# Fused Fourier mixing and MLP mixer on one Trainium2 core: re-planning the setup and moving the Nyquist column from TensorE to VectorE

## The chip, the cores and the metric

One core of a Trainium2 chip. The metric is the device time of one execution in microseconds (us). The profile is one execution; its "span" runs from the first to the last instruction and is about 1.8 us shorter than the device time of the same execution. The kernel's matrix products run on TensorE (PE in the profile, PEld is its weight loads), the copies, adds and activations on VectorE (DVE), ScalarE (ACT) and GpSimd (POOL). GpSimd and SyncE (SP) also issue the data transfers.

Executions differ, mostly by 1 to 2 us, by up to 3.5 us for the kernel before (642.22 to 645.68). The profiles below point to TensorE's granted clock in the first 50 us; that it explains every such difference is not shown, since only one execution of each run was profiled.

## The reference

```
X = fft(fft(x, axis=1), axis=2).real            # x: 8 x 3008 x 256
h = relu(X.transpose(0,2,1) @ w_tok1) @ w_tok2  # w_tok1: 3008 x 256, w_tok2: 256 x 3008
u = X + h.transpose(0,2,1)
out = u + relu(u @ w_ch1) @ w_ch2               # w_ch1: 256 x 1536, w_ch2: 1536 x 256
```

## The kernel before

All eight batches go through the core one after the other. The work of a batch has two parts.

- The **front** computes the Fourier transform and the token products: z products (short transforms along the sequence), the d stage (the transform along the 256 features, 12 groups), the token products with w_tok1 already carried through the transform tables (tiles hp and hq), the third stage (py, pq) and the products with w_tok2 (pu). It ends in the tile ut.
- The **channel part** has 24 sub-steps per batch. Each is one group of first channel products (mm1: six products of 512 columns) and one of second channel products (mm2: twelve of 256 columns).

The front of batch b+1 is a generator whose steps are handed out between the sub-steps of batch b by a plan. Before all this there is a **setup**: angle tables tp and tq (sines), small tables for z (t1n, t1b) and for the d stage (td0, td1), the load of the first batch x0 and its **fold** on VectorE (sums and differences of mirrored rows), and hp and hq.

The order of the setup, shortened:

```python
    r3 = []
    for off in (offp, offq):                         # angles of tp and tq, both on VectorE
        m3 = gen.tile([P, 768], FP32, ...)
        ts(m3[:], kb[:], reff[:], AT.mult, off[:], AT.add)
        r3.append(reduced(m3[:], S, P, 768))          # three more VectorE operations
    table3(tp, r3[0]); turn(tp, tts_p, 12)            # sines on ScalarE, transposes on TensorE
    table3(tq, r3[1]); turn_rows(tts_p, 1.0, 8)
    pl = nc.gpsimd
    ...                                               # t1n, t1b: on GpSimd (eng=pl)
    turn(tq, tts_q, 24); turn_rows(tts_q, -1.0, 0)
    ...                                               # td0, td1, perm: on GpSimd
    load_wc()
    take(fold(0, [nc.vector] * 4), 4)
    x_tiles[1] = load_x(1)
    own = front(0)
    take(own, 4); carried(tts_p, hp)                  # carried: 24 products with w_tok1
    take(own, 4); carried(tts_q, hq)
    take(own, 19)                                     # d stage, token products, third stage, first pu
```

The d stage and the third stage, in `front(b)`:

```python
        for g in range(NG):                           # NG = 12
            pw = ps_f("pw")                           # one of three PSUM buffers
            ...
            nc.tensor.matmul(pw[:, 0:WD], lhsT=zb, rhs=td1[:], start=True, stop=False)   # 259 columns
            nc.tensor.matmul(pw[:, 0:131], lhsT=za, rhs=td0[:], start=False, stop=True)
            copy(g % 2 and b == 0, w[:, g, :], pw[:, 0:WD])
            yield
        ...
        for c in range(3):                            # third stage, all chunks ahead of pu
            ...
            yield
```

The plan, and the end of the last batch in `mm2` (ks counts the four row blocks of a chunk):

```python
    plan = [[0] * 11 + [3, 3, 2, 4, 4, 4, 1, 1, 2, 1, 4, 4, 4], ...]   # steps of the next front per sub-step
    ...
        if ks % 2 == 0:
            box["po"] = ps_out("po")                  # one PSUM tile for two row blocks
        ...
        if ks % 2 == 1:                               # VectorE adds for two blocks at once
            ...
        if ks == 3:                                   # stores for four blocks
```

## Time and profile before

| | before |
|---|---|
| time, three runs | 642.7 us (642.53 to 643.55) |
| PE busy | 618.1 us, 96% of the span |
| first channel product starts | 44.57 us |
| batch 0, to batch 1's first channel product | 79.87 us |
| one batch, mean from batch 2 to batch 7 | 74.54 us |
| from batch 7's start to the end of the span | 71.68 us |

From the page of the profile: busy time by engine, the tenths of TensorE's busy time and granted clock in 40 slices, and the chain of work that ended last.

```profile
PE 618.1 (96%) x4778; PEld 425.6 (66%) x4778; DVE 330.4 (51%) x702; ACT 317.4 (49%) x667; POOL 251.0 (39%) x250
PE   3789999999999999999999999999999999999996
PEclk9779999999999999999999999999999999999999
PE 93%; POOL 2%; DVE 2%; ACT 1%; issue 1%; DVEq 0%; POOLq 0%; ACTq 0%
```

TensorE bounds the kernel, and only the first three slices (48 us) and the last show anything else. The view of stretches says it sharper. Its columns are the stretch, its length, then busy time of PE, PEld, DVE, ACT and POOL (number of instructions in brackets), the granted clock, the share of the DMA engines and GB/s.

```profile
40.00:50.00 10.00, 8.82 (x34) 3.62 (x34) 6.76 (x12) 4.63 (x9) 2.98 (x2) 0.66 0.80 178
140.00:600.00 460.00, 460.00 (x3564) 318.05 (x3563) 233.01 (x487) 224.82 (x483) 148.53 (x130) 1.00 0.41 78
```

Between 140 and 600 us TensorE is never idle, so there only TensorE work that is taken away can save time. At 40 to 50 us its mean clock is 0.66.

A caution for every clock figure. The clock records of a profile begin when the clock is first raised, 13.5 to 25.5 us into the span in the profiles here. Ahead of that the views print 1.00, but the spacing of the products shows half clock. In the kernel before the first record is at 13.48 us, and twelve products of 128 columns take 1.46 us ahead of it and 0.83 us after it:

```profile
9.85 1.46 PE L266 MATMUL pt<-ident,tp 128*128 128x128 f16 x12 [9.85 <-ACT tp L235]
...
14.03 0.83 PE L266 MATMUL pt<-ident,tq 128*128 128x128 f16 x12
```

So a mean clock of 1.0 over a whole span speaks only of the time after the first record.

TensorE in the timeline: start, length, engine, line, operation, tiles. First a d group (two products) in the steady part and the first product of the next, then the first channel products, then the last 48 products of the kernel.

```profile
138.05 0.27 PE L443 MATMUL pw<-td_305,z 128*128 128x259 f16 x1
138.16 0.22 PE L444 MATMUL pw<-td_304,z 128*128 128x131 f16 x1
138.22 0.27 PE L443 MATMUL pw<-td_305,z 128*128 128x259 f16 x1
...
44.57 2.88 PE L539 MATMUL pc<-ut,wc1p 128*128 128x512 f16 x6 [0.43 <-DVE ut L514]
...
631.57 5.40 PE L560 MATMUL po<-wc_148,c_7866 128*128 128x256 f16 x48
```

Lengths of products overlap; the distance between starts is what a product costs: 0.11 us for 259 columns and 0.06 us for 131. The six first channel products take 2.88 us, where later ones take 1.46: that is the half clock.

VectorE in the timeline, the start and end of the fold of x0:

```profile
11.10 0.68 DVE L394 TENSOR_TENSOR xd<-xp,xm 94x1024 f16<-94x1024 f16 x1
11.81 0.69 DVE L395 TENSOR_TENSOR xp<-xp,xm 94x1024 f16<-94x1024 f16 x1
...
20.00 0.58 DVE L403 TENSOR_TENSOR eo<-xd 94x635 f16<-94x635 f16 x1
```

### The profile page before, as it was taken

How to read it: one execution, taken by the hardware profiler on the slowest of the kernel's cores; microseconds unless marked ns; L12 is line 12 of the kernel's file. 1: busy time of each engine (PE TensorE's matmuls, PEld its weight loads, DVE VectorE, ACT ScalarE, POOL GpSimd, SP SyncE). 2: the span in 40 equal slices, each digit the busy share in tenths (PEclk: the TensorE clock that was granted, in tenths of full speed). 3: DMA queues.
4: the chain of work that ended last, by engine and by line, in shares of the span. 5: the costliest groups of instructions: out<-in, count | busy, mean ns of one | idle time of the engine just before them, and what ended most of it. 6: DMA issues, size and time to landing. Idle time of an engine off the chain costs nothing.

```text
span 642.6 us, 11805 instructions
## 1 busy us (share of the span) xinstructions
PE 618.1 (96%) x4778; PEld 425.6 (66%) x4778; DVE 330.4 (51%) x702; ACT 317.4 (49%) x667; POOL 251.0 (39%) x250
## 2 busy tenths in 40 slices
PE   3789999999999999999999999999999999999996
PEld 3545667567666776667766676667766777666665
DVE  8755435733664447633565336643466336653442
ACT  7547465265535554365534645356533655334431
POOL 8819869659130880059411691039400000000000
PEclk9779999999999999999999999999999999999999
DMA  9992462732922268142853239323221522533332
GB/s 148 177 215 52 92 140 51 149 60 55 161 67 67 58 93 149 33 101 56 130 74 78 66 61 140 82 66 83 58 51 34 115 51 50 67 74 70 80 82 66
DMA packets 86550, 56.28 MB, mean 88 GB/s; under 512 B 54832, under 2 KB 83440, under 8 KB 85744
## 3 DMA queue, kind: packets, MB, share of 16 engines
q1 hardware_dynamic: 78240, 38.04, 28.5%
q0 software_dynamic: 8256, 17.49, 17.1%
q8 instruction: 37, 0.61, 0.4%
q14 instruction: 17, 0.14, 0.1%
HBM read 34.98 MB, written 24.64 MB: 93 GB/s over the span
## 4 chain that ended last, share of the span: by engine, by line
PE 93%; POOL 2%; DVE 2%; ACT 1%; issue 1%; DVEq 0%; POOLq 0%; ACTq 0%
PE po L560 38%; PE pc L539 38%; PE pu L506 6%; PE pw L443 2%; PE pz L416 1%; PE pw L444 1%; PE py L482 1%; PE pq L482 1%; PE ph L363 0%; DVE yt L487 0%; DVE ut L514 0%; PE ph L365 0%; PE pz L432 0%; POOL xm L118 0%; PE pz L426 0%
## 5 line engine op out<-in xcount | busy, mean ns | idle before, releaser
L539 PE MATMUL pc<-ut,wc1p 128*128 128x512 f16 x576 | 141.3, 381 | 0.5 <-DVE ut L514 0.4
L539 PE MATMUL pc<-ut,wc1m 128*128 128x512 f16 (+1 forms) x576 | 134.9, 370 | 0.0
L574 DVE TENSOR_TENSOR osb<-po,rt 128x258 f32<-128x258 f32 (+3 forms) x240 | 74.6, 361 | 55.9 <-PE po L560 51.5
L539 PEld LDWEIGHTS <-wc1m 128*128 128x128 f16 x576 | 54.8, 98 | 54.0
L539 PEld LDWEIGHTS <-wc1p 128*128 128x128 f16 x576 | 53.2, 98 | 51.8 <-issue 5.7
L514 DVE TENSOR_TENSOR ut<-pu,yt 128x512 f16<-128x512 f32 (+1 forms) x96 | 61.5, 670 | 35.6 <-PE pu L506 35.6
L394 POOL TENSOR_TENSOR xd<-xp,xm 94x1024 f16<-94x1024 f16 x28 | 59.3, 2119 | 19.7 <-DMA xm<-in_x_dram,ix_76 19.7
L395 POOL TENSOR_TENSOR xp<-xp,xm 94x1024 f16<-94x1024 f16 x28 | 59.3, 2119 | 2.2
L399 POOL TENSOR_TENSOR eo<-xp 94x512 f16<-94x512 f16 (+1 forms) x28 | 34.0, 1213 | 61.6 <-PE pz L432 60.3
L291 ACT ACTIVATE w<-pw 128x259 f16<-128x259 f32 x90 | 30.1, 386 | 49.6 <-PE pw L444 49.1
L291 ACT ACTIVATE z<-pz 128x480 f16<-128x480 f32 (+1 forms) x59 | 34.5, 674 | 24.7 <-PE pz L416 20.5
L506 PE MATMUL pu<-w2p,uu 128*128 128x512 f16 (+1 forms) x168 | 45.0, 379 | 0.5 <-DVE ut L514 0.5
L487 DVE TENSOR_TENSOR yt<-py,qs 128x512 f16<-128x512 f32 x48 | 30.6, 685 | 18.9 <-ACT qs L485 9.4
L592 POOL COPY ch<-c_7196 128x768 f16<-128x768 f16 x1 | 0.8, 825 | 86.0 <-DVE c_7196 L87 86.0
L403 POOL TENSOR_TENSOR eo<-xd 94x508 f16<-94x508 f16 (+1 forms) x28 | 33.8, 1205 | 0.0
L506 PEld LDWEIGHTS <-uu 128*128 128x128 f16 x192 | 19.0, 99 | 11.7 <-issue 2.7
L485 ACT ACTIVATE qs<-pq 128x512 f32<-128x512 f32 x24 | 14.1, 595 | 19.4 <-PE pq L482 9.2
L443 PE MATMUL pw<-td_305,z 128*128 128x259 f16 x96 | 21.4, 274 | 0.9 <-ACT w L291 0.6
L594 POOL COPY c_7866<-ch 128x768 f16<-128x768 f16 x1 | 0.8, 828 | 50.8 <-PE po L560 50.8
L444 PE MATMUL pw<-td_304,z 128*128 128x131 f16 x96 | 18.8, 221 | 0.0
L474 ACT ACTIVATE uu<-uv 128x256 f16<-128x256 f32 (+2 forms) x48 | 13.2, 337 | 9.9 <-DVE uv L469 9.9
L128 POOL DMA_DIRECT2D xp<-in_x_dram x32 | 17.2, 561 | 0.2 <-issue 0.2
(429 smaller groups left out, 1146.8 us busy)
## 6 DMA issues: line engine op xcount, KB each, us to landing
out_dram<-osb SPq DMA_DIRECT2D x84, 256.0 KB, 3.7
xp<-in_x_dram POOLq DMA_DIRECT2D x16, 272.0 KB, 5.6
out_dram<-osb SPq DMA_DIRECT2D x12, 192.0 KB, 2.8
xp<-in_x_dram POOLq DMA_DIRECT2D x16, 127.5 KB, 6.2
rt<-ut SPq DMA_TRANSPOSE x96, 2.7
w2s<-in_moe_w_tok_dram POOLq DMA_DIRECT2D x1, 1504.0 KB, 18.3
w1p<-in_moe_w_tok_dram POOLq DMA_DIRECT2D x2, 384.0 KB, 9.6
wc_148<-in_moe_w_ch_dram POOLq DMA_DIRECT2D x1, 768.0 KB, 12.1
```

Of the source, the lines that this page charges most:

```text
L291: nc.scalar.activation(out=out_, in_=in_, func=AFT.Copy)
L394: eng.tensor_tensor(out=xd[:, t, :], in0=xp[:, t, :], in1=rv, op=AT.subtract)
L395: eng.tensor_tensor(out=xp[:, t, :], in0=xp[:, t, :], in1=rv, op=AT.add)
L399: eng.tensor_tensor(out=eo[:, t, 1:129], in0=xp[:, t, 1:129], in1=xp[:, t, 255:127:-1], op=AT.add)
L403: eng.tensor_tensor(out=eo[:, t, 129:256], in0=xd[:, t, 1:128], in1=xd[:, t, 255:128:-1], op=AT.subtract)
L443: nc.tensor.matmul(pw[:, 0:WD], lhsT=zb, rhs=td1[:], start=True, stop=False)
L487: nc.vector.tensor_tensor(out=yt[:, h, CW * c:CW * c + CW], in0=py[:], in1=qs[:], op=op)
L506: nc.tensor.matmul(pu[:, 0:n], lhsT=uu[:, th, int(minus), h, :], rhs=w2_cols(b, c)[:, th], start=(th == 0), stop=(th == 1))
L514: nc.vector.tensor_tensor(out=ut[:, h, f0:f0 + n].rearrange("p (a b) -> p a b", b=64), in0=pu[:, 0:n].rearrange("p (b a) -> p a b", b=64), ...
L539: nc.tensor.matmul(pc[:, 0:n], lhsT=wc[:, h, ct * P:(ct + 1) * P], rhs=ut[:, h, f0:f0 + n], start=(h == 0), stop=(h == 1))
L560: nc.tensor.matmul(po[0:n, o:o + D], lhsT=c1[:, ct, ks * P:ks * P + n], rhs=wc2[:, ct, :], start=(ct == 0), stop=(ct == NCT - 1))
L574: nc.vector.tensor_tensor(out=osb[r, ks_, j], in0=src[r, k0:k1, j], in1=rt[r, ks_, p], op=AT.add)
```

## The change

The intent has five parts.

1. **Nyquist by VectorE.** The d stage's first product had 259 columns only because one Nyquist value with alternating sign was added to 131 columns by the product. Now it has 128 columns, and VectorE adds the alternating row.
2. **Setup.** The small tables (t1n, t1b, td) go to VectorE, where they fill the wait for x0; the angles of tq go to GpSimd; the d stage is dealt out among the products with w_tok1.
3. **Clock.** 24 filler products stand ahead of the first channel product.
4. **Plan.** The third stage is made one chunk at a time, ahead of the pu products of its chunk; eleven steps of batch 1's front move from batch 0 into batch 1; half of a sub-step's steps go ahead of mm2.
5. **Tail.** In the last chunk of the last batch every row block is added by itself, and the stores go out in two halves on two queues.

The core of the diff (cuts marked `...`):

```diff
-    r3 = []
-    for off in (offp, offq):
-        ...
+    ts(m1[0:KR, 0:48], kf[0:KR, 0:48], qcol[0:KR, :], AT.mult, 47 / 4, AT.add)     # eng=pl dropped, as in
+    ...                                                                            # all small tables
+    table3(tp, angles3(offp, nc.vector))
+    ...                                                  # ident, anti, md, td0, td1, t1n, t1b on VectorE
+    r3q = angles3(offq, pl)                              # tq's angles on GpSimd
+    load_wc()
...
-            nc.tensor.matmul(pw[:, 0:WD], lhsT=zb, rhs=td1[:], start=True, stop=False)
-            nc.tensor.matmul(pw[:, 0:131], lhsT=za, rhs=td0[:], start=False, stop=True)
-            copy(g % 2 and b == 0, w[:, g, :], pw[:, 0:WD])
+            nc.tensor.matmul(pw[:, 131:WD], lhsT=zb, rhs=td1[:], start=True, stop=True)
+            nc.tensor.matmul(pw[:, 0:131], lhsT=za, rhs=td0[:], start=True, stop=True)
+            copy(0, w[:, g, 132:WD], pw[:, 132:WD])
+            nc.vector.scalar_tensor_tensor(
+                out=w[:, g, 0:131], in0=alt[:], scalar=pw[:, 131:132],
+                in1=pw[:, 0:131], op0=AT.mult, op1=AT.add)
...
+        final = last and b + 1 == BB
+        if ks % 2 == 1 or final:
...
+                parts = [(slice(0, n), ks % 2, ks % 2 + 1)]
...
+        if ks == 3 or (final and ks == 1):
...
+    take(fold(0, [nc.vector] * 4), 4)
+    own = front(0)
+    take(own, 2)
+    filler(16)
+    table3(tq, r3q)
+    take(own, 2)
+    turn(tq, tts_q, 0)
+    take(own, 2)
+    turn_rows(tts_q, -1.0, 0)
+    take(own, 2)
+    for g2 in range(NG // 2 + 1):
+        if g2 < NG // 2:
+            take(own, 2)
+            carried(tts_p, hp, g2, 0)
+        if g2 > 0:
+            carried(tts_q, hq, g2 - 1, g2 % 3 > 0)
+    take(own, 5)
+    filler(24)
...
+    plan = [[0] * 11 + [2, 2, 2, 2, 3, 3, 3, 3, 1, 1, 1, 2, 1],
+            [2] * 10 + [1, 1, 1, 2, 1, 2, 1, 2, 1, 1, 1, 1, 1, 1]]
...
+                if sub < 12:
+                    take(own, 1)
+                take(nxt, n // 2)
                 if prev is not None:
                     mm2(*prev, s, pbox)
...
+                take(nxt, n - n // 2)
```

More of the change, by code (lines that the diff above doesn't have):

```diff
@@ L235, in sin @@
         nc.scalar.activation(out=out_, in_=in_, func=AFT.Sin, scale=scale)
-    ident = const.tile([P, P], FP16, tag="ident")
-    anti = const.tile([P, P], FP16, tag="anti")
-    acol = pvec("acol")
-    ts(acol[:], pcol[:], -1.0, AT.mult, 127.0, AT.add)
-    ts(ident[:], jrow[:, 0:P], pcol[:], AT.is_equal)
-    ts(anti[:], jrow[:, 0:P], acol[:], AT.is_equal)
-    r3 = []
-    for off in (offp, offq):
-        m3 = gen.tile([P, 768], FP32, tag="m3", bufs=2, name="m3")
-        ts(m3[:], kb[:], reff[:], AT.mult, off[:], AT.add)
-        r3.append(reduced(m3[:], S, P, 768))
     def table3(tab, r):
@@ L263, in turn @@
         for h in range(2):
-            pt = ps_f("pt", FP16, 1024)
+            pt = psum.tile([P, 1024], FP16, tag="mm", name="pt", bufs=3)
             for g in range(6):
@@ L291, in copy @@
             nc.scalar.activation(out=out_, in_=in_, func=AFT.Copy)
-    tts_p, tts_q = turned(), turned()
-    table3(tp, r3[0])
-    turn(tp, tts_p, 12)
-    table3(tq, r3[1])
-    turn_rows(tts_p, 1.0, 8)
     pl = nc.gpsimd
     mask0, q24 = pvec("mask0"), pvec("q24")
-    ts(mask0[:], xicol[:], -1.0, AT.mult, 1.0, AT.add, eng=pl)
-    ts(q24[:], qcol[:], 24.0, AT.add, eng=pl)
+    ts(mask0[:], xicol[:], -1.0, AT.mult, 1.0, AT.add)
+    ts(q24[:], qcol[:], 24.0, AT.add)
     t1n = const.tile([KR, 2, 2, 24], FP16, tag="t1n")
@@ L307 @@
     kf = krow[:].rearrange("p a k -> p (a k)")
-    ts(m1[0:KR, 0:48], kf[0:KR, 0:48], qcol[0:KR, :], AT.mult, 47 / 4, AT.add, eng=pl)
-    ts(m1[0:KR, 48:96], kf[0:KR, 48:96], qcol[0:KR, :], AT.mult, eng=pl)
-    ts(m1[0:KR, 96:120], kf[0:KR, 0:24], q24[0:KR, :], AT.mult, 47 / 8, AT.add, eng=pl)
-    r1 = reduced(m1[0:KR, :], 47, KR, 120, pl)
+    ts(m1[0:KR, 0:48], kf[0:KR, 0:48], qcol[0:KR, :], AT.mult, 47 / 4, AT.add)
+    ts(m1[0:KR, 48:96], kf[0:KR, 48:96], qcol[0:KR, :], AT.mult)
+    ts(m1[0:KR, 96:120], kf[0:KR, 0:24], q24[0:KR, :], AT.mult, 47 / 8, AT.add)
@@ L312, with angles3 @@
+    r1 = reduced(m1[0:KR, :], 47, KR, 120)
     cs = gen.tile([P, 120], FP32, tag="cs")
     sin(cs[0:KR, :], r1, PI2 / 47)
+    def angles3(off, eng):
+        m3 = gen.tile([P, 768], FP32, tag="m3", bufs=2, name="m3")
+        ts(m3[:], kb[:], reff[:], AT.mult, off[:], AT.add, eng=eng)
+        return reduced(m3[:], S, P, 768, eng)
+    table3(tp, angles3(offp, nc.vector))
+    ident = const.tile([P, P], FP16, tag="ident")
+    anti = const.tile([P, P], FP16, tag="anti")
+    acol = pvec("acol")
@@ new lines @@
+    ts(acol[:], pcol[:], -1.0, AT.mult, 127.0, AT.add)
+    ts(ident[:], jrow[:, 0:P], pcol[:], AT.is_equal)
+    ts(anti[:], jrow[:, 0:P], acol[:], AT.is_equal)
+    md = gen.tile([P, 255], FP32, tag="md")
+    ts(md[:, 0:128], jrow[:, 1:129], pcol[:], AT.mult, 64.0, AT.add)
+    ts(md[:, 128:255], jrow[:, 1:128], pcol[:], AT.mult)
+    rd = reduced(md[:], 256, P, 255)
+    td0 = const.tile([P, 131], FP16, tag="td0")
+    td1 = const.tile([P, P], FP16, tag="td1")
+    alt = const.tile([P, 131], FP16, tag="alt")
@@ L314 @@
+    sin(td0[:, 2:130], rd[:, 0:128], PI2 / 256)
+    sin(td1[:, 1:P], rd[:, 128:255], PI2 / 256)
     csv = cs[0:KR, 0:96].rearrange("p (a b k) -> p a b k", a=2, b=2)
     for i, m in ((0, mask0), (1, xicol)):
-        ts(t1n[:, :, i, :], csv[:, :, i, :], m[0:KR, :], AT.mult, eng=pl)
+        ts(t1n[:, :, i, :], csv[:, :, i, :], m[0:KR, :], AT.mult)
     ts(t1b[:, 1, :], cs[0:KR, 96:120], float(np.sqrt(0.5)), AT.mult,
-       xicol[0:KR, :], AT.mult, eng=pl)
-    pl.tensor_copy(out=t1b[:, 0:3:2, :], in_=t1n[:, :, 0, :])
@@ L321 @@
-    turn(tq, tts_q, 24)
-    turn_rows(tts_q, -1.0, 0)
-    md = gen.tile([P, 255], FP32, tag="md")
-    ts(md[:, 0:128], jrow[:, 1:129], pcol[:], AT.mult, 64.0, AT.add, eng=pl)
-    ts(md[:, 128:255], jrow[:, 1:128], pcol[:], AT.mult, eng=pl)
-    rd = reduced(md[:], 256, P, 255, pl)
-    td0 = const.tile([P, 131], FP16, tag="td0")
-    td1 = const.tile([P, WD], FP16, tag="td1")
-    sin(td0[:, 2:130], rd[:, 0:128], PI2 / 256)
-    sin(td1[:, 132:WD], rd[:, 128:255], PI2 / 256)
+       xicol[0:KR, :], AT.mult)
@@ L335 @@
+    nc.vector.tensor_copy(out=t1b[:, 0:3:2, :], in_=t1n[:, :, 0, :])
+    r3q = angles3(offq, pl)
+    load_wc()
     pl.memset(td0[:, 0:1], 1.0)
@@ L338 @@
     ts(td0[0:1, :], td0[0:1, :], 0.5, AT.mult, eng=pl)
-    pl.memset(td1[:, 0:132], 0.0)
-    pl.memset(td1[0:1, 0:2], 0.5)
-    pl.memset(td1[0:1, 3:130:2], 0.5)
-    pl.memset(td1[0:1, 2:130:2], -0.5)
+    pl.memset(td1[:, 0:1], 0.0)
+    pl.memset(td1[0:1, 0:1], 0.5)
+    pl.memset(alt[:], 1.0)
+    pl.memset(alt[:, 2:129:2], -1.0)
+    pl.memset(alt[:, 130:131], 0.0)
     tcol, sgn = pvec("tcol"), pvec("sgn")
@@ L351, with carried @@
     ts(perm[:], jrow[:, 0:P], tcol[:], AT.is_equal, sgn[:], AT.mult, eng=pl)
+    tts_p, tts_q = turned(), turned()
     hp = const.tile([P, NG, DTOK], FP16, tag="hp")
     hq = const.tile([P, NG, DTOK], FP16, tag="hq")
-    def carried(tts, dst):
-        for g2 in range(NG // 2):
-            ph = ps_mm("ph")
-            for k in range(2):
-                g = 2 * g2 + k
-                o = ph[:, k * DTOK:(k + 1) * DTOK]
-                nc.tensor.matmul(o, lhsT=tts[0][:, g * P:g * P + P], rhs=w1p[:, g, :],
-                                 start=True, stop=False)
-                nc.tensor.matmul(o, lhsT=tts[1][:, g * P:g * P + P], rhs=w1m[:, NG - 1 - g, :],
-                                 start=False, stop=True)
-            copy(g2 % 2, dst[:, 2 * g2:2 * g2 + 2, :].rearrange("p g k -> p (g k)"),
-                 ph[:])
+    def carried(tts, dst, g2, e):
+        ph = ps_mm("ph")
+        for k in range(2):
+            g = 2 * g2 + k
+            o = ph[:, k * DTOK:(k + 1) * DTOK]
+            nc.tensor.matmul(o, lhsT=tts[0][:, g * P:g * P + P], rhs=w1p[:, g, :],
+                             start=True, stop=False)
+            nc.tensor.matmul(o, lhsT=tts[1][:, g * P:g * P + P],
+                             rhs=w1m[:, NG - 1 - g, :], start=False, stop=True)
+        copy(e, dst[:, 2 * g2:2 * g2 + 2, :].rearrange("p g k -> p (g k)"), ph[:])
     w2v = w2s[:].rearrange("p h (b a) -> p h b a", a=NQ)
@@ L419, in front @@
                 zo = z[:, half, :, :].rearrange("p k (u s) -> p u k s", u=4)
-                copy(b == 0 and (half == 0 or t0 == 11), zo[:, :, :, t0:t0 + 5],
+                copy(b == 0 and t0 == 1, zo[:, :, :, t0:t0 + 5],
                      pz[:, 0:480].rearrange("p (t u k) -> p u k t", t=5, u=4))
@@ L476, in front, with third @@
         yt = perb.tile([P, 2, HALF], FP16, tag="yt", name="yt")
-        for c in range(3):
+        def third(c):
             py, pq = ps_f("py"), ps_f("pq")
@@ L488, in front @@
                                         in1=qs[:], op=op)
-            yield
         ut = perb.tile([P, 2, NCH * CW], FP16, tag="ut", name="ut", bufs=2)
@@ L499, in front @@
         for c in range(NCH):
+            if c < 3:
+                third(c)
+                yield
             f0 = CW * c
@@ L562, in mm2 @@
                              start=(ct == 0), stop=(ct == NCT - 1))
-        if ks % 2 == 1:
+        final = last and b + 1 == BB
+        if ks % 2 == 1 or final:
             src = po[:].rearrange("p (k d) -> p k d", k=2)
@@ L566, in mm2 @@
                                                           (slice(0, n), 1, 2)]
+            if final:
+                parts = [(slice(0, n), ks % 2, ks % 2 + 1)]
             for r, k0, k1 in parts[0:2 if n else 1]:
-                ks_ = slice(ks - 1 + k0, ks - 1 + k1)
+                ks_ = slice(ks - ks % 2 + k0, ks - ks % 2 + k1)
                 adds = [(slice(minus, P + 1 - minus), slice(minus, P + 1 - minus)),
@@ L575, in mm2 @@
                                             in1=rt[r, ks_, p], op=AT.add)
-        if ks == 3:
+        first = 2 if final and ks == 3 else 0
+        if ks == 3 or (final and ks == 1):
             for i in range(2):
-                nk = 3 if last and (i or n == 0) else 4
-                nc.sync.dma_start(
-                    out=dram(out_t, (b * S + 8 * c + i) * D,
-                             [[NQ * D, 64], [2 * D, nk], [1, D]]),
-                    in_=osb[64 * i:64 * i + 64, 0:nk, :])
-            if last and b % 2:
+                nk = min(ks + 1, 3 if last and (i or n == 0) else 4)
+                eng = nc.scalar if i and final else nc.sync
+                eng.dma_start(
+                    out=dram(out_t, (b * S + 8 * c + i + 2 * first) * D,
+                             [[NQ * D, 64], [2 * D, nk - first], [1, D]]),
+                    in_=osb[64 * i:64 * i + 64, first:nk, :])
+            if ks == 3 and last and b % 2:
                 nc.sync.dma_start(
@@ L599, in take @@
             next(g, None)
-    load_wc()
+    turn(tp, tts_p, 8)
+    turn_rows(tts_p, 1.0, 24)
     take(fold(0, [nc.vector] * 4), 4)
+    own = front(0)
[15 more added lines that the diff above has]
+    filler(24)
     if BB > 1:
         x_tiles[1] = load_x(1)
-    own = front(0)
-    take(own, 4)
-    carried(tts_p, hp)
-    take(own, 4)
-    carried(tts_q, hq)
-    take(own, 19)
-    for h in range(2):
-        swap_wc1(h)
-    if BB > 1:
         take(fold(1, [nc.gpsimd] * 4), 4)
@@ L618 @@
     work = ctx.enter_context(tc.tile_pool(name="work", bufs=1))
-    plan = [[0] * 11 + [3, 3, 2, 4, 4, 4, 1, 1, 2, 1, 4, 4, 4],
-            [2] * 4 + [2] * 6 + [1, 1] + [1] * 3 + [1, 2] * 4 + [0]]
+    plan = [[0] * 11 + [2, 2, 2, 2, 3, 3, 3, 3, 1, 1, 1, 2, 1],
+            [2] * 10 + [1, 1, 1, 2, 1, 2, 1, 2, 1, 1, 1, 1, 1, 1]]
     prev = None
@@ L632 @@
                 sub = 4 * c + s
+                n = plan[b > 0][sub]
                 mm1(b, c, c1, range(3 * s, 3 * s + 3))
+                if sub < 12:
+                    take(own, 1)
+                take(nxt, n // 2)
                 if prev is not None:
                     mm2(*prev, s, pbox)
-                if b == 0:
-                    if s % 2 == 0:
-                        take(own, 1)
-                    if sub < 8:
-                        align_w2(sub)
-                n = plan[b > 0][sub]
-                take(nxt, n)
+                if b == 0 and sub < 8:
+                    align_w2(sub)
+                take(nxt, n - n // 2)
                 done += n
@@ L647 @@
                     turned_u[b + 1, 0] = turn_u(b + 1, 0)
+                if b == 0 and sub == 3:
+                    for h in range(2):
+                        swap_wc1(h)
                 if done >= 8 and not folded:
@@ L656 @@
             prev, pbox = (b, c, c1), box
+        own = nxt
     for s in range(4):
```

## The prediction

> **What bounds it.** TensorE. The page gives PE 618.1 of 642.6 us (96%), and PE is 93% of the chain that ended last; VectorE is 51% busy, ScalarE 49%. The table of stretches shows no PE idle time from 140 to 600 us. So between those times only removed TensorE work counts. From batch 2 to batch 7 one batch takes 74.5 us (starts 198.20 and 570.92 in the timeline); my sum of its spacings is 74.2, so hidden stalls are small. The rest is at the edges: the first channel product starts at 44.57 us, batch 0 takes 79.9 us (to 124.44) where its products alone need about 74.9, and after the last product (636.97) 5.6 us pass.
>
> **Step 1, Nyquist by VectorE: -4.6 us.** The d stage's pair has 259 and 131 columns; they start 0.110 and 0.057 us apart. With 128 columns the first needs about 0.056 (TensorE: Matmul & The Clock Gate, "Back-to-back issue gap", N/2.4 + 2.5 ns; the trace's own 128-column products start 0.056 apart, so it agrees). 0.054 x 12 groups x 7 batches = 4.6 us, all on the critical path. It adds 96 VectorE operations of 131 columns, estimated at 0.28 us like the 127-column subtract (27 us in all), and shortens 96 ScalarE copies of 0.386 to about 0.27. Both engines have room.
>
> **Step 2, setup: -3.5 us.** Small tables move to VectorE before the fold, which starts some 0.5 us later (11.6). tq goes to GpSimd (about 4 to 5 us, ready near 16, no wait). Between 12 and 25 us ScalarE becomes the limit: transposed tables, z copies, tq sines, about 12 us of work. The d stage starts near 25, and six steps (two d groups, four w_tok1 products of each table) take about 1.3 us each, by ScalarE copies. The folded-token products then end near 36 (before 37.43). From there to the first channel product it took 7.1 us, with three third-stage chunks in a VectorE/ScalarE chain; with one chunk about 5.2. First channel product near 41 instead of 44.57. Two third chunks (0.9 us of PE) only move into batch 0.
>
> **Step 3, clock: -1.5 us.** The first six channel products start 0.43 us apart, later ones 0.216: half clock (the same page, Part 1: an idle window throttles; the trace's granted clock is 0.66 in 40 to 50 us). Fillers before them should keep full clock.
>
> **Step 4, batch 0: -2 us.** Its stalls besides the clock are about 3.5 us: groups of four d products wait for w copies, thirds for qs, pu for ut. The new plan issues them singly around mm2. Eleven steps of batch 1's front (4.7 us) move to the next batch, which is neutral. x1 should land no later than before (46.9), so the GpSimd fold doesn't stall z.
>
> **Step 5, tail: -1 us.** The last adds cover one row block (0.82 to about 0.55 us) and one of three 0.6 us store issues goes to another queue.
>
> Sum: -4.6 - 3.5 + 0.9 - 1.5 - 2 - 1 = -11.7: **631 us**, range 627 to 636. Chances: faster by over 2% 0.36, within 2% 0.62, slower 0.02.
>
> **What would show it.** Step 1: d products 0.056 apart and a batch period near 73.9. Step 2: first channel product at 39.5 to 42.5. Step 3: granted clock near 1.0 in 40 to 50 us, first channel products 0.216 apart. Step 4: PE idle in batch 0 under 1.5 us. Step 5: under 4.8 us after the last product.
>
> **What would make it wrong.** GpSimd slower than estimated (tq or the alternating row late); ScalarE queueing longer in setup; x1 landing after 50 us, which stalls z; the VectorE operation slow enough that three PSUM buffers stall TensorE; or a setup that overlaps better than I think, which takes it past 2%.

## The result, and the profile after

The changed kernel took 635.91 us (median of 4 runs, 635.72 to 635.92) against 643.12 us before (642.53 to 645.12) on the same chip: ratio 0.9882, 95% interval 0.9859 to 0.9904. Ratios here are the mean time of one kernel's fast runs over that of the other's of the same rounds, so they are not quite the ratio of the medians quoted. The time lies at the upper edge of the predicted range: 1.2% faster, where 1.8% was forecast (11.7 of 642.7 us). The profiled executions differ by 8.5 us (spans 642.6 and 634.1), the medians by 7.2: the profiled execution of the kernel before took 644.38 us and was 1.3 us slower than the median, so about 1.3 us of the parts below belong to that execution, in which part is not known. The starts of the batches, read from the timeline, cut this difference into parts that add up:

| part | before | after | measured | predicted |
|---|---|---|---|---|
| to the first channel product | 44.57 | 43.23 | -1.34 | -3.5 |
| batches 0 and 1 | 153.63 | 149.11 | -4.52 | -3.9 |
| batches 2 to 6 | 372.72 | 369.53 | -3.19 | -3.2 |
| batch 7 and the end | 71.68 | 72.23 | +0.55 | -1.0 |
| sum | | | -8.50 | -11.6 |

(The predicted value for batches 0 and 1 is its sum of: step 1 for two fronts, -1.3; the clock, -1.5; the stalls, -2; the two third chunks that moved in, +0.9. Steps have to be put to batches this way because eleven front steps moved from batch 0 to batch 1. The parts give -11.6 instead of the prediction's -11.7 by rounding. Spans are printed to 0.1 us, so the parts after batch 7's start are good to 0.05 us.)

Two of the four parts came in near the prediction. The first and the last did not: 2.2 us short in the setup, 1.5 us in the tail.

From the page, and from the view of stretches:

```profile
PE 610.8 (96%) x4806; PEld 422.4 (67%) x4806; DVE 356.7 (56%) x807; ACT 315.8 (50%) x677; POOL 248.7 (39%) x238
PE   2789999999999999999999999999999999999996
PEclk9999999999999999999999999999999999999999
40.00:50.00 10.00, 9.16 (x61) 4.64 (x62) 6.59 (x11) 6.57 (x14) 6.33 (x5) 1.00 0.50 102
140.00:600.00 460.00, 460.00 (x3581) 316.71 (x3579) 253.92 (x558) 221.23 (x479) 140.62 (x124) 1.00 0.44 79
```

The clock is now full from 40 to 50 us, and PE is still never idle in the long middle. TensorE in the timeline, the same three places as before:

```profile
128.95 0.22 PE L442 MATMUL pw<-td_190,z 128*128 128x128 f16 x1
129.00 0.22 PE L443 MATMUL pw<-td_189,z 128*128 128x131 f16 x1
129.06 1.47 PE L566 MATMUL po<-wc_148,c_1652 128*128 128x256 f16 x12
...
43.23 0.38 PE L545 MATMUL pc<-ut,wc1p 128*128 128x512 f16 x1
43.83 1.24 PE L545 MATMUL pc<-ut,wc1p 128*128 128x512 f16 x5 [0.22 <-DVE ut L520]
...
622.52 1.47 PE L566 MATMUL po<-wc_148,c_7994 128*128 128x256 f16 x12
624.64 2.78 PE L566 MATMUL po<-wc_148,c_7994 128*128 128x256 f16 x24 [0.65 <-DVE osb L583]
628.06 1.47 PE L566 MATMUL po<-wc_148,c_7994 128*128 128x256 f16 x12 [0.65 <-DVE osb L583]
```

A d group now costs 0.11 us instead of 0.17. The first channel products run at full clock. The last 48 products, 5.40 us in one piece before, now stop twice for VectorE (osb is the output tile of the adds) and take 7.0 us (622.52 to 629.53).

VectorE in the setup (first six lines), and GpSimd at the same time (last four):

```profile
11.99 1.08 DVE L231 TENSOR_TENSOR gr<-gv,md 128x255 f32<-128x255 f32 x1
13.00 0.81 DVE L87 TENSOR_SCALAR t1n<-cs,mask_149 94x48 f16<-94x48 f32 x1
13.87 0.84 DVE L89 TENSOR_SCALAR t1b<-cs,xicol 94x24 f16<-94x24 f32 x1
14.71 0.68 DVE L393 TENSOR_TENSOR xd<-xp,xm 94x1024 f16<-94x1024 f16 x1
15.42 2.18 DVE L394 TENSOR_TENSOR xp<-xp,xm 94x1024 f16<-94x1024 f16 x1
24.75 0.48 DVE L402 TENSOR_TENSOR eo<-xd 94x635 f16<-94x635 f16 x1
...
11.69 1.11 POOL L89 TENSOR_SCALAR m_198<-kb,reff,offq 128x768 f32<-128x768 f32 x1
12.88 0.88 POOL L226 TENSOR_SCALAR gv<-m_198 128x768 f32<-128x768 f32 x1
13.85 0.84 POOL L228 TENSOR_SCALAR gv<-gv 128x768 f32<-128x768 f32 x1
14.77 2.28 POOL L231 TENSOR_TENSOR gr<-gv,m_198 128x768 f32<-128x768 f32 x1
```

This is the finding of the comparison. The fold starts at 14.71 us where the prediction had 11.6, and ends at 25.23 instead of 20.58. Add start and length on both engines: t1n ends at 13.81, GpSimd's second operation at 13.76; t1b at 14.71, the third at 14.69; the first xp add at 17.60, the fourth at 17.05. An xp add took 0.69 us before and takes 2.18 us here. VectorE seems to stand still until GpSimd's operation is over.

### The profile page after: what moved, and what is told of

It reads as the page before. It is cut to its first block, busy times and chain, and to the rows that moved or that the text cites. A ratio compares the mean times of both kernels' runs of the same rounds, so it can differ in the third digit from the quotient of the medians.

```text
span 634.1 us, 11971 instructions
## 1 busy us (share of the span) xinstructions
PE 610.8 (96%) x4806; PEld 422.4 (67%) x4806; DVE 356.7 (56%) x807; ACT 315.8 (50%) x677; POOL 248.7 (39%) x238
## 4 chain that ended last, share of the span: by engine, by line
PE 92%; issue 1%; ACT 1%; DVE 0%; DVEq 0%; ACTq 0%
PE po L566 39%; PE pc L545 38%; PE pu L512 6%; PE pz L415 1%; PE py L485 1%; PE pq L485 1%; PE pw L443 1%; PE pw L442 1%; PE pz L431 0%; PE pz L425 0%; ACT c_714 L548 0%; DVE osb L583 0%; PE pt_5989 L457 0%; PE pt_4067 L457 0%; PE pt_3176 L457 0%
## 5 line engine op out<-in xcount | busy, mean ns | idle before, releaser
L583 DVE TENSOR_TENSOR osb<-po,rt 128x258 f32<-128x258 f32 (+4 forms) x246 | 75.2, 356 | 50.2 <-PE po L566 44.1
L520 DVE TENSOR_TENSOR ut<-pu,yt 128x512 f16<-128x512 f32 (+1 forms) x96 | 64.4, 672 | 19.7 <-PE pu L512 19.7
L276 ACT ACTIVATE z<-pz 128x480 f16<-128x480 f32 (+1 forms) x61 | 39.7, 668 | 27.1 <-PE pz L415 22.0
L512 PE MATMUL pu<-w2p,uu 128*128 128x512 f16 (+1 forms) x168 | 50.0, 379 | 0.0
L276 ACT ACTIVATE w<-pw 128x127 f16<-128x127 f32 x96 | 25.8, 280 | 47.0 <-PE pw L443 47.0
L445 DVE SCALAR_TENSOR_TENSOR w<-alt,pw 128x131 f16<-128x131 f16 x96 | 32.8, 351 | 18.6 <-ACT w L276 18.6
L442 PE MATMUL pw<-td_190,z 128*128 128x128 f16 x96 | 20.4, 220 | 0.9 <-DVE z L274 0.7
L415 PEld LDWEIGHTS <-eo 94*128 94x128 f16 x240 | 15.8, 101 | 7.9 <-DVE eo L400 2.5
L415 PE MATMUL pz<-t1n,eo 94*128 94x96 f16 x240 | 18.6, 211 | 2.1 <-DVE eo L400 2.1
```

The source lines that it names most:

```text
L276: nc.scalar.activation(out=out_, in_=in_, func=AFT.Copy)
L415: nc.tensor.matmul(pz[:, 96 * k:96 * k + 96], lhsT=eo[:, t0 + k, c], rhs=t1n[:].rearrange("p a b k -> p (a b k)"), start=True, stop=True)
L445: nc.vector.scalar_tensor_tensor(out=w[:, g, 0:131], in0=alt[:], scalar=pw[:, 131:132], in1=pw[:, 0:131], op0=AT.mult, op1=AT.add)
L512: nc.tensor.matmul(pu[:, 0:n], lhsT=uu[:, th, int(minus), h, :], rhs=w2_cols(b, c)[:, th], start=(th == 0), stop=(th == 1))
L520: nc.vector.tensor_tensor(out=ut[:, h, f0:f0 + n].rearrange("p (a b) -> p a b", b=64), in0=pu[:, 0:n].rearrange("p (b a) -> p a b", b=64), ...
L583: nc.vector.tensor_tensor(out=osb[r, ks_, j], in0=src[r, k0:k1, j], in1=rt[r, ks_, p], op=AT.add)
```

## The experiments

Theory A: GpSimd's operations for tq hold up VectorE. Its rivals: x0 lands late, or VectorE simply has more to do. Theory B: the tail lost by its own new waits. Further: what is step 1 worth alone, do the fillers hold the clock, and which part of the new plan removed the stalls. All kernels gave the right result except where it is said.

The table gives the time, the ratio to the kernel before run beside it with its 95% interval, and from the profiled execution the first channel product, batch 0, the part from batch 7's start, and the span. All kernels with the Nyquist change have 73.89 to 73.91 us per batch from batch 2 to batch 7.

| run | time | ratio | first product | batch 0 | last part | span |
|---|---|---|---|---|---|---|
| changed kernel | 635.91 | 0.9882 (0.9859 to 0.9904) | 43.23 | 71.23 | 72.23 | 634.1 |
| changed kernel again | 635.21 | 0.9863 (0.984 to 0.9886) | 42.98 | 71.24 | 72.27 | 633.9 |
| Nyquist only | 641.75 | 0.9959 (0.9939 to 0.9979) | 45.58 | 80.59 | 71.65 | 640.4 |
| no tq angles (wrong result) | 632.36 | 0.9827 (0.9803 to 0.985) | 39.18 | 71.23 | 72.28 | 630.1 |
| tq angles on VectorE | 634.61 | 0.9853 (0.9836 to 0.9869) | 41.92 | 71.24 | 72.34 | 632.9 |
| no fillers | 636.91 | 0.9883 (0.9866 to 0.9899) | 44.11 | 72.50 | 72.28 | 636.3 |
| tail with own PSUM tiles | 634.28 | 0.9855 (0.9829 to 0.9881) | 42.44 | 71.23 | 70.63 | 631.7 |
| tq early | 635.41 | 0.9859 (0.9834 to 0.9885) | 43.58 | 71.23 | 72.28 | 634.5 |
| all mended | 632.65 | 0.9822 (0.9799 to 0.9845) | 41.72 | 71.23 | 70.74 | 631.1 |
| all mended, warm | 631.27 | 0.981 (0.9794 to 0.9825) | 40.16 | 71.23 | 70.70 | 629.5 |
| all mended, warmer | 632.39 | 0.9827 (0.9811 to 0.9842) | 41.29 | 71.23 | 70.67 | 630.6 |
| front after mm2 | 635.75 | 0.9884 (0.9864 to 0.9904) | 42.62 | 71.21 | 72.24 | 633.4 |
| groups of four | 638.73 | 0.9918 (0.9896 to 0.9939) | 44.25 | 73.83 | 72.29 | 637.7 |

A caution on the column "first product": the tail, plan and filler experiments share the changed kernel's setup up to the d stage, and still their first channel product moves between 42.44 and 44.25 us. Two things go with it. The fold ends at 24.7 us in these four profiles and at 25.2 in the changed kernel's own two. And in the two latest (44.11 and 44.25) TensorE ran at half clock from 21 to 31 us. Differences under a microsecond in that column are not evidence by themselves.

### Nyquist only

The kernel before with step 1 alone:

```diff
...                                  # td1 with 128 columns, alternating row alt
-            nc.tensor.matmul(pw[:, 0:WD], lhsT=zb, rhs=td1[:], start=True, stop=False)
-            nc.tensor.matmul(pw[:, 0:131], lhsT=za, rhs=td0[:], start=False, stop=True)
-            copy(g % 2 and b == 0, w[:, g, :], pw[:, 0:WD])
+            nc.tensor.matmul(pw[:, 131:WD], lhsT=zb, rhs=td1[:], start=True, stop=True)
+            nc.tensor.matmul(pw[:, 0:131], lhsT=za, rhs=td0[:], start=True, stop=True)
+            copy(0, w[:, g, 132:WD], pw[:, 132:WD])
+            nc.vector.scalar_tensor_tensor(out=w[:, g, 0:131], in0=alt[:], ...)
```

> The kernel before with step 1 alone (128-column d product, alternating row added by VectorE). Theory: the d stage's PE work shrinks by 0.054 us per group on the critical path of seven batches, so the batch period from batch 2 to batch 7 falls from 74.5 to about 73.9 us and the time by 4.6 us, to about 638. Rival: most of the 7.5 us of the whole change is this step (8 batches and fewer stalls on the w copies in batch 0), then 6 us or more; or the 96 VectorE operations stall PE through the three PSUM buffers, then under 3 us.

The batch period is as expected (73.89 us). But the time fell only by the ratio's 0.4%, about 2.6 us. The rest went back at the two places where the d stage is not spread out: the first channel product came 1.0 us later, and batch 0 took 80.59 us instead of 79.87, although its first channel products here ran at full clock. The list of waits of TensorE shows 1.7 us in three waits of d products for VectorE's add, the longest 0.8 us, which the kernel before does not have, and its longest wait of a pu product for the ut adds is 1.3 us instead of 0.3. So step 1's worth on the critical path was right where it was computed, in the steady part; it needs the new plan to be worth that elsewhere.

### No tq angles

The cleanest test of theory A: GpSimd's four operations for tq are gone, and tq uses tp's angles. The result is wrong; everything else runs as before.

```diff
-    table3(tp, angles3(offp, nc.vector))
+    r3p = angles3(offp, nc.vector)
+    table3(tp, r3p)
...
-    r3q = angles3(offq, pl)
+    r3q = r3p
```

> The changed kernel without the tq angle operations on GpSimd (tq takes tp's angles; the result is wrong on purpose). Theory: GpSimd operations that read SBUF make VectorE operations wait to their end, so without them t1n and t1b take under 0.35 us instead of 0.81 and 0.84, the first xp add about 0.7 instead of 2.18, the fold ends near 22.6 instead of 25.23 us, the d stage starts near 26 instead of 28.5, and the kernel is about 2.3 us faster than the changed one (633.6). Rival: the fold is late because x0 lands late or because VectorE simply has more to do; then the xp add stays near 2.2 us, the fold ends at 24.7 us or later and the time stays within 0.5 us of 635.9.

VectorE in the timeline of this run, the operations shown above:

```profile
11.21 0.42 DVE L231 TENSOR_TENSOR gr<-gv,md 128x255 f32<-128x255 f32 x1
11.55 0.24 DVE L87 TENSOR_SCALAR t1n<-cs,mask 94x48 f16<-94x48 f32 x1
11.86 0.31 DVE L89 TENSOR_SCALAR t1b<-cs,xicol 94x24 f16<-94x24 f32 x1
12.26 0.69 DVE L394 TENSOR_TENSOR xd<-xp,xm 94x1024 f16<-94x1024 f16 x1
12.98 0.69 DVE L395 TENSOR_TENSOR xp<-xp,xm 94x1024 f16<-94x1024 f16 x1
...
21.05 0.48 DVE L403 TENSOR_TENSOR eo<-xd 94x635 f16<-94x635 f16 x1
```

Each operation has its own length again: 0.42 for 1.08 us, 0.24 for 0.81, 0.31 for 0.84, 0.69 for 2.18. These four differences are 3.25 us, and the fold ends 3.7 us earlier (21.53 for 25.23). The first channel product comes 4.05 us earlier (the 0.35 us beyond the fold's may be the clock, whose first record is at 15.91 us here and at 23.65 in the changed kernel), and the ratio is lower by 0.55%, about 3.5 us; against the second run of the changed kernel it is 0.36%, with intervals that overlap slightly. Theory A is shown, and stronger than expected; x0 was there in time, since the fold could start at 12.26. It also shows the rest of the prediction's setup to have been sound: with the fold nearly where the prediction had it, the d stage starts at 24.43 (predicted "near 25") and the first channel product at 39.18 (predicted 41).

The Trainium skill has the rule that the prediction missed. "SBUF — State Buffer", section "Who interferes with whom", says that VectorE and GpSimd share one pair of SBUF ports, that an operation of either that needs the pair holds it for its whole length, and that one of the other's that needs it too then waits. The ends of the operations above agree with it.

### tq angles on VectorE

```diff
-    r3q = angles3(offq, pl)
+    r3q = angles3(offq, nc.vector)
```

> The changed kernel with the tq angles on VectorE just ahead of the fold, as their kernel before had them on VectorE (right result). Theory: the VectorE operations stretched by GpSimd (2.6 us in all) go back to their own length, but 3.05 us of angles come in their place, so the fold ends between 25 and 26 us and the time is within 0.7 us of 635.9: the move to GpSimd gave VectorE nothing. Rival: the move was worth its 3 us on VectorE; then the fold ends at 28 us and the time is 638 or more.

VectorE now does 3 us more work ahead of the fold, and the fold still ends earlier: at 24.08 us instead of 25.23 in the changed kernel's profile (24.74 in the profile with the least collision of the same setup). The ratio's interval, 0.9836 to 0.9869, overlaps that of both runs of the changed kernel, so the gain in time is not settled; that the move to GpSimd gained nothing is. The rival, that the move was worth its 3 us on VectorE, falls.

### No fillers

```diff
     take(own, 5)
-    filler(24)
```

> The changed kernel without the 24 fillers ahead of the first channel product. Theory of the prediction: PE then idles about 3 us between 40 and 44 us, falls to half clock, and the first channel products start 0.43 us apart for some 3 us: 1.3 to 1.5 us slower (637.3). Rival: PE was so busy from 28 to 39 us that gaps of 0.9, 0.4 and 2 us don't lower the clock; then the granted clock in 40 to 50 us stays near 1.0 and the time stays within 0.3 us of 635.9.

In the profiled execution batch 0 took 72.50 us instead of 71.23, and the granted clock was 0.70 and 0.73 in the stretches 44 to 47 and 47 to 50 us. That is the expected 1.3 us. The time is inconclusive: the ratio equals the changed kernel's. The four executions ran from 636.58 to 638.08 us, and the mean clocks of their whole spans from 0.989 to 0.996. The later first channel product of this profile (44.11) is not the fillers' doing: the clock was already 0.50 from 23 to 29 us, well ahead of the place of the change. The same happened in the groups-of-four run, which has the fillers: 0.50 from 23 to 29 us, a first product at 44.25, but clock 1.00 from 44 to 50 us. So the fillers do their local work in an execution like this one. They are not always needed: the Nyquist-only run has none, and its clock was 1.00 from 41 to 50 us. How often an execution needs them these runs don't settle.

### Tail with own PSUM tiles

Each of the last four row blocks gets a PSUM tile of its own, so no product has to wait until VectorE has read a tile's other half.

```diff
-        if ks % 2 == 0:
+        final = last and b + 1 == BB
+        if final:
+            box["po"] = (ps_out if ks < 2 else ps_mm)("po")
+        elif ks % 2 == 0:
             box["po"] = ps_out("po")
         po = box["po"]
-        o = D * (ks % 2)
+        o = 0 if final else D * (ks % 2)
...
```

> The changed kernel with each of the last four row blocks in a PSUM tile of its own. Theory: the changed tail lost because the second block of a PSUM tile waits for VectorE to have read the first (two waits of 0.65 us, PE 7.0 instead of 5.4 us for the last 48 products); with own tiles the waits go, the last 48 products take 5.4 us again, and the span falls by 1.5 us to about 632.5. Rival: the waits are hidden behind the stores or the rt load, then the span stays within 0.4 us of the changed kernel.

The last part fell from 72.23 to 70.63 us, 1.6 us, as expected. The last 60 products now run in one piece, in TensorE's timeline of this run:

```profile
620.41 6.71 PE L569 MATMUL po<-wc,c 128*128 128x256 f16 x60
```

Compared with the kernel before (71.68), the tail's idea is then worth -1.05 us, the -1.0 of the prediction. The ratio by itself does not show it: two of the four executions took 633.5 us and two 635.1, the latter two with mean clocks of 0.994 and 0.991 instead of 0.997. The last part's 1.6 us repeats in the three mended kernels (70.67 to 70.74).

### tq early, and all mended

In the tq-on-VectorE run ScalarE idles 4.4 us ahead of the first z copies, and from there works almost without a gap into the d stage. Two kernels follow. The first moves tq's sines, transposes and mirrored rows into that hole:

```diff
     turn_rows(tts_p, 1.0, 24)
+    table3(tq, r3q)
+    turn(tq, tts_q, 8)
+    turn_rows(tts_q, -1.0, 16)
     take(fold(0, [nc.vector] * 4), 4)
...                                  # taken out of their old places after the fold, filler(8) put there
```

> The kernel with tq angles on VectorE (e3), and with tq's sines, transposes and mirrored rows ahead of the z copies in the order of ScalarE and TensorE. Theory: in e3 ScalarE idles 4.4 us before the first z copies (15.3 to 19.8 us) and then runs without a gap into the d stage; filling that hole starts the d stage near 25.7 instead of 27.4 us and the first channel product near 40.2 instead of 41.9, span 631.2. Rival: the fold alone sets the d stage's start; then the first channel product stays within 0.5 us of 41.9.

The second also makes tq's angles from tp's reduced angles, since the two differ by 0 or a quarter turn per row, and takes over the tail above:

```diff
-    r3q = angles3(offq, pl)
+    ts(wrap[:], r3p, thr[:], AT.is_lt, float(S), AT.mult)
+    nc.vector.scalar_tensor_tensor(out=r3q[:], in0=r3p, scalar=offd[:], in1=wrap[:],
+                                   op0=AT.add, op1=AT.add)
...
```

> The changed kernel with all mends: tq early in the order, its angles on VectorE made from tp's reduced angles by two operations (about 1.5 us in place of 3.05), and own PSUM tiles in the tail. Theory: first channel product near 38.7 us, last 48 products 5.4 us, span about 628.2, ratio 0.978 to the kernel before. Rival: another limit takes over in setup (ScalarE or the d tables from GpSimd), then the first channel product stays above 39.7 us.

Both missed their first channel product, by 3.4 and 3.0 us. In "tq early" the d stage did start earlier (26.71 us instead of the 27.18 with tq's angles on VectorE), but then its six steps with the w_tok1 products took 9.4 us instead of 7.3. The view of stretches for "all mended" says why (columns as before, clock third from last):

```profile
23.00:26.00 3.00, 1.36 (x15) 1.00 (x14) 1.50 (x3) 1.14 (x4) 1.58 (x4) 1.00 1.04 215
26.00:29.00 3.00, 2.83 (x21) 2.15 (x19) 1.75 (x5) 2.01 (x8) 0.00 (x0) 0.63 1.02 201
29.00:32.00 3.00, 3.00 (x28) 2.50 (x27) 1.94 (x6) 2.09 (x6) 1.68 (x2) 0.80 1.24 198
```

With tq's work gone from there, TensorE was busy only 1.36 of the 3 us ahead of the d stage, and then ran it at half clock in part. Of the four executions of "tq early" one shows a mean clock of 1.0: it took 633.88 us, the others 635.26 to 636.40.

### All mended, warm and warmer

The same kernel with more fillers between and after the last z products:

```diff
     filler(8)
-    take(own, 4)
+    take(own, 2)
+    filler(10)
+    take(own, 1)
+    filler(10)
+    take(own, 1)
+    filler(16)
```

> e8 with 10, 10 and 16 more fillers between and after the last z products. Theory: in e8 and e7 TensorE idled in pieces from 22.7 to 25.8 us and fell to half clock for the first half of the d stage and w_tok1 products (9.3 us in place of 7.1 us in e7), which ate the earlier start; with the gaps filled the six steps take about 7.1 us at full clock, the first channel product is near 39.8 us in place of 41.7, the span near 629.2 and the ratio about 0.979. Rival: those steps are limited by copies on ScalarE and VectorE, not by the clock; then they take 9 us again and the time stays within 0.5 us of e8.

> The same with 16, 16 and 24 fillers. Theory: the clock holds more surely, but the fillers outlast the gaps by up to 0.9 us; within 1 us of e11, first channel product near 40.3 us.

The view of stretches for "all mended, warm":

```profile
23.00:26.00 3.00, 3.00 (x50) 2.70 (x48) 1.52 (x3) 1.05 (x3) 1.60 (x4) 1.00 0.99 205
26.00:29.00 3.00, 2.82 (x33) 2.49 (x31) 2.40 (x8) 2.72 (x9) 0.00 (x0) 1.00 1.04 206
29.00:32.00 3.00, 2.93 (x33) 2.57 (x31) 2.29 (x7) 2.79 (x10) 1.80 (x2) 1.00 1.21 205
```

The clock holds, the first channel product is at 40.16 us, and the five executions lie between 631.26 and 631.33 us, mean clocks 0.998 to 1.0. The spread of a microsecond or two that most of the other kernels show is gone here, and so are the dips of the clock in the profile. This kernel beats both the kernel before (by 1.9%) and the changed one. Its lead over "all mended" (a ratio of 0.981 against 0.9822, first product 1.56 us earlier) is shown by the profile and by separate ranges of times, 631.3 against 632.1 to 632.8, from different calls; the intervals of the ratios overlap. The "warmer" kernel lost 1.1 us: its d stage starts at 26.67 us instead of 25.54, behind the added fillers, and it is as steady (632.38 to 632.41).

### Front after mm2, and groups of four

Which part of the new plan keeps batch 0 free of stalls? First, all front steps after mm2 again:

```diff
-                take(nxt, n // 2)
                 if prev is not None:
                     mm2(*prev, s, pbox)
...
-                take(nxt, n - n // 2)
+                take(nxt, n)
```

> The changed kernel with all front steps after the second channel product, in groups of up to three, as the kernel before had them in groups of up to four, instead of half of them ahead of it. Theory: the groups wait on the copies of the d products and the ut adds, so batch 0 (71.23 us) grows by 0.5 to 2 us and PE shows idle time there again; later batches (groups of two) stay at 73.9 us on average. Rival: the spreading was worth nothing; then batch 0 stays within 0.2 us of 71.23.

Nothing changed: batch 0 took 71.21 us. The expectation fell. Splitting the steps around mm2, which the prediction named as what would help, was worth nothing. Then the same with the twelve d groups of batch 1 in three runs of four, as the kernel before had them, instead of four runs of three:

```diff
-    plan = [[0] * 11 + [2, 2, 2, 2, 3, 3, 3, 3, 1, 1, 1, 2, 1],
+    plan = [[0] * 11 + [2, 2, 2, 2, 4, 4, 4, 0, 1, 1, 1, 2, 1],
```

> The kernel of e10 with batch 1's twelve d products in three groups of four instead of four groups of three. Theory, after e10: not the split around the second channel product but the group size against three PSUM buffers is what counts; a fourth group in a row waits for the copies of the first. Then PE waits about 0.5 to 0.7 us in each of three groups and batch 0 takes 72.5 to 73.5 us instead of 71.21. Rival: VectorE's queue in batch 0 of the kernel before (adds of the third stage and of ut), not the group size, made those waits; then batch 0 stays within 0.3 us of 71.21.

Batch 0 took 73.83 us, 2.6 us more. TensorE in the timeline of this run, the fourth group of each four, with its wait in square brackets:

```profile
90.67 0.22 PE L442 MATMUL pw<-td,z 128*128 128x128 f16 x1 [0.77 <-DVE w L445]
94.42 0.22 PE L442 MATMUL pw<-td,z 128*128 128x128 f16 x1 [0.53 <-DVE w L445]
98.48 0.22 PE L442 MATMUL pw<-td,z 128*128 128x128 f16 x1 [0.83 <-DVE w L445]
```

There are three PSUM buffers. A fourth group in a row has to wait until the first is read out, and since step 1 that takes two readers in turn, the ScalarE copy and then VectorE's add (0.35 us; in the changed kernel the groups of operations show it waiting for ScalarE's copy of w, 18.6 us in 23 waits). The new plan's groups of three just fit. But this is the cost of groups of four together with step 1. In the kernel before, where a single copy reads each group, the fourth groups of batch 0 waited only 0.31, 0.14 and 0.31 us, of 1.9 us of idle time of TensorE there. The other waits were mostly for the ut adds and qs; which part of the plan removed those was not tested.

## Why the prediction was right or wrong

- **Bound and direction: right.** TensorE's work bounds the kernel, and the gain is in the edges and in removed columns. By the medians 7.2 of the expected 11.7 us came.
- **Step 1, 0.054 us per group: right in the steady part.** The period fell by 0.63 us per batch (74.54 to 73.91; 0.65 predicted). The VectorE operation was under-sized (0.35 us, not 0.28), which did not matter at the new plan's group size. By itself the step gave 2.6 us, not 4.6: its prediction holds only with the plan.
- **Step 2, "the fold starts some 0.5 us later (11.6)" and "tq goes to GpSimd (about 4 to 5 us, ready near 16, no wait)": this is the step that failed.** tq was ready at 17.05 and nobody waited for its data. But the operations themselves stopped VectorE: the fold started at 14.71 us and ended 4.65 us later than before. The prediction costed a move between engines by each engine's busy time, as if the two were independent. Without these operations the fold started at 12.26 and the first channel product was at 39.18. The setup gave -1.34 instead of -3.5 us.
- **Step 3, the clock: right in mechanism.** Full clock from 40 to 50 us; without fillers 1.27 us more in batch 0 of the one execution profiled. In the time of whole executions it could not be separated.
- **Step 4, -2 us: about right in its sum, wrong in its reason.** PE's idle time in batch 0 fell from 1.9 to 0.4 us, as predicted (under 1.5), and batches 0 and 1 gave -4.52 instead of -3.9 us, which also holds steps 1 and 3. But the split around mm2 gained nothing (71.21 against 71.23 us). Smaller groups kept step 1 from costing 2.6 us; of the kernel before's own stalls they account for some 0.8 us, and what removed the rest stays open.
- **Step 5, -1 us: wrong sign, +0.55.** The prediction counted the shorter adds and the second queue and missed that two row blocks share a PSUM tile, so the second block's products now wait for the first one's adds. With own tiles the tail gave -1.05 us, the predicted -1. The prediction's own check for this step, under 4.8 us after the last product, came true (4.6 us) while the tail got slower: the time was lost ahead of the last product, where the check did not look.
- **What could make it wrong.** The list named slow GpSimd and late tables, not GpSimd's effect on VectorE, which was the cause.

What stays open: the collisions of GpSimd and VectorE come in two patterns for the same setup code (fold begun at 14.7 us in two profiles of the changed kernel, at 13.0 in the four other profiles that share its setup, with ends of 25.2 and 24.7), and what decides between them is not known. The VectorE operations at 9 to 11 us are also slow (md 1.35 us in the changed kernel, 0.28 in the "all mended" kernel) while GpSimd only issues transfers; but it issues them in both kernels, so that alone is not the reason, and the reason is not known.

## What to carry to other kernels

Work that is moved to an idle engine can still slow the engine it was taken from: before moving SBUF work to GpSimd, compare what VectorE does in the same microseconds, and look for VectorE operations that end just when GpSimd's do. When work is taken out of a setup, look at TensorE's clock again in the hole that is left, and fill it. A steady time from run to run is no proof that the clock holds: the changed kernel's first four runs lie within 0.2 us, and its profiled execution ran at half clock until 23.65 us. Deal out PSUM-filling steps in groups no larger than the number of buffers, and when a split makes results ready sooner, check that the halves don't share a PSUM tile.

## What the Trainium skill lacked or had wrong

- "TensorE: Matmul & The Clock Gate" tells the reader, in the table of "Why this matters for your kernels", to avoid PE-idle gaps longer than about 3 us. Keeping to that was not enough here: in the "all mended" kernel no idle gap of TensorE between 22.7 and 25.8 us is over 0.7 us (1.1 in "tq early"), and the clock still fell (0.63 in the next 3 us) after a stretch in which it was busy 1.36 of 3.00 us. In the changed kernel 2.00 of 3.00 us kept it at 1.00.
- No page says what share of busy time keeps the clock. In these traces each spell of full or half clock that ends in the first 50 us lasts 3.41 us or two, three or four times that. Cut into such steps from its first clock record on, the first 60 us of the 14 profiles have 11 steps at full clock with TensorE busy for 0.77 to 1.97 us, all followed by half clock, and 153 steps with 2.00 us or more, none followed by it. This is no general rule: near the end of the changed kernel (627.8 to 631.2 us) a step with 1.47 us was still followed by full clock.
- "SBUF — State Buffer", "Who interferes with whom", has the rule of the shared ports right, and the trace agrees (an xp add of 0.69 us took 2.18 us and ended 0.55 us after GpSimd's operation). It gives no example of small operations in a row: here three table operations of 0.24 to 0.42 us took 0.81 to 1.08 us one after the other, each beside a GpSimd operation.
- The same page's warning about transfers issued by GpSimd describes VectorE holding up the issue. Whether such issues hold up VectorE no run here tested: beside them md took 1.35 us in the changed kernel, but 0.28 us in "all mended" (from 9.24 us, with an issue from 9.07 to 9.93).
